# Eight PSUM tiles of one bank in place of four of two, in a kernel of causal attention and a two-layer feed-forward net

## The chip, the core and the metric

The program runs on one core of a Trainium2 chip. Its time is the device time of one execution in microseconds (us), median of three runs. Five engines work side by side, each through a queue of its own in the order written: TensorE (PE in the profile, its weight loads PEld), VectorE (DVE), ScalarE (ACT), GpSimd (POOL) and SyncE (SP, which here only issues DMAs). PSUM, where TensorE writes, has eight banks of 512 float32 columns in each of 128 partitions.

## What is computed

Eight batches, eight heads, 576 tokens, head size 64. Per head: scores `q k^T / 8` plus a decay `cum[s] - cum[t]` (`cum` is the running sum of `log f`), causal mask, softmax over the keys, times `v`. The heads side by side are the 4608 x 512 matrix x of the net:

```python
h = x @ w_in                                        # 512 x 2048
g = np.maximum(h, 0.0) + alpha * np.minimum(h, 0.0)
return (g @ w_out).astype(np.float32)               # 2048 x 512
```

All float32. The large products are made from a high and a low part of each factor (three matmuls of kind fp32r, called the three terms below).

## The kernel before

**Pairs of heads.** The 64 heads are done as 32 pairs n, the two heads of a pair in the two halves of the partitions. Pairs 0 to 9 (`attention`, line 546) turn their weights with TensorE. Pairs 10 to 31 (`turned`, line 800) turn them with VectorE and DMAs. The 576 queries are four blocks of 128 (i = 0 to 3) and a tail of 64; the tails of both heads share one block of 128 rows.

**A turned pair.** TensorE first makes the scores of blocks 3, 2 and 0 of both heads (`run1`, line 850) into four banks: `bA` holds block 3, one bank for each head, `bB` blocks 2 and 0 of a head in one bank. `shrink` (832) follows for each block and head: on VectorE one pass adds the decay and finds the row's minimum (line 840; its accumulator is then read by a short instruction), on ScalarE `expo` makes the exponentials and their sum (820). Then `run2` (873) makes the tail (two halves of 288 keys in the two banks of `bD`) and block 1 (256 columns in each bank of `bC`), again followed by two `shrink` and by `tail` (889; 576 columns in one VectorE pass, line 891). Right behind `run2` TensorE runs `values` (915) of an earlier pair: the product of its turned weights with v, which is x of that pair before division. Its blocks 0 to 3 (t < 4, two batches of 256 columns) go to columns 256 to 511 of the two banks of `bC`, beside block 1 of the present pair, and its tail (t = 4, 64 columns) to columns 320 to 383 of a bank of `bD`, beside the present tail. ScalarE copies x out (938, 940). `turn` (861) is the VectorE transpose of the weights, in two pieces (line 863), and sixteen DMAs (line 900) move the pieces on.

**The net.** `ffn1` (995) multiplies 512 tokens with 128 columns of `w_in`: 12 matmuls of 512 columns into one bank, issued as two halves of six. The bank is emptied by ScalarE (line 1015, or 1012 for the token groups 0, 7 and 8, where that is all) and then by VectorE (1017), and a DMA stores the result (1019). Its matmuls fill TensorE's time between the steps of the pairs. `ffn2` (1224) runs at the end: 18 units of 256 tokens, each with four banks of its own, made by seven products in place of eight and put together by ScalarE and VectorE (lines 1298 to 1315). w_out is converted for it between the pairs' end and its start (1169).

**Banks and order.** The pool of PSUM is four tiles of two banks (line 254); `banks` is a store of the eight halves, and rings (`rS`, `rT`, `rH`, `rO`, `rV`) take single banks from it, each with a least and a most number that it may hold. `rH` (for `ffn1`) holds 2 to 4. When the last plain pair is through, `swap_banks` (1071) claims banks 0 to 3, and whole tiles of two go to the ring `rP` of the turned pairs; `change` (1118) gives them back behind the last pair. The order of all instructions is made by a planner (`Plan.run`, 143): every operation has an assumed duration, a key and its dependencies; the operation with the earliest possible start of all engines is written next (lines 153 to 180), and takes the bank that has been free for longest. The waits between the engines are put in afterwards by the framework, from the accesses to each tile in the order written.

```python
two_banks = [psum.tile([128, 2, 512], F32, name=f"bank{i}") for i in range(4)]
banks = Store([t[:, i] for t in two_banks for i in range(2)])
...
rP, rV = Ring(pairs), Ring(banks, 0, 2)
```

Of the kernel before, what the change touches and what calls it, by code (L numbers as in the profile page):

```python
# [48 lines left out]
class Store:  # L49


    def __init__(self, items):
        self.items, self.rings = items, []
        self.free = [(0.0, i) for i in range(len(items))]
        self.claimed = None

    def take(self):

        f = min(self.free)
        self.free.remove(f)  # L60
        return f

    def give(self, t, i):

        if self.claimed and i in self.claimed[0]:
            self.claimed[1](t, i)
        else:
            self.free.append((t, i))

    def claim(self, which, fn):  # L70

        self.claimed = (which, fn)
        mine, self.free = [f for f in self.free if f[1] in which], [f for f in self.free if f[1] not in which]
        for t, i in mine:
            fn(t, i)

# [34 lines left out]
class Plan:  # L111
# [31 lines left out]
    def run(self):  # L143
# [7 lines left out]
        while left:  # L151
# [40 lines left out]
            for b in o.bufs:  # L192
                if b.t is not None:
                    continue
                st = b.ring.store
                f = st.take()
                b.i, b.t = f[1], st.items[f[1]]
                if o.eng == "PE" and st is self.banks:
                    new.append((f[0], b.t))
                b.ring.next += 1  # L200
                b.ring.held += 1
# [3 lines left out]
            for b in o.bufs:  # L205
                b.left -= 1
                b.last = max(b.last, end)
                if b.left == 0:
                    b.ring.held -= 1
                    b.ring.store.give(b.last + 0.3, b.i)  # L210
            for c in o.outs:
# [7 lines left out]
def attention_moe(  # L219
# [33 lines left out]
    psum = ctx.enter_context(tc.tile_pool(name="psum", bufs=1, space=PSUM))  # L253
    two_banks = [psum.tile([128, 2, 512], F32, name=f"bank{i}") for i in range(4)]
    banks = Store([t[:, i] for t in two_banks for i in range(2)])
    pairs = Store([])
    plan.banks = banks
# [11 lines left out]
    rH, rO = Ring(banks, 2, 4), Ring(banks, 0, 6)  # L269
    rP, rV = Ring(pairs), Ring(banks, 0, 2)  # L270
    rx = Ring(Store([xx[:, 1024 * i : 1024 * i + 1024].rearrange("p (k q) -> p k q", k=2) for i in range(7)]))
# [528 lines left out]
    def turned(n):  # L800
# [8 lines left out]
        bE1, bE2, bTt, bM, bst, bxs, bri = Buf(rE), Buf(rE2), Buf(rEt), Buf(rM), Buf(rst), Buf(rxs), Buf(rri)  # L809
        lo, su = (lambda: bst.t[:, 16:25]), (lambda: bst.t[:, 0:9])  # L810
        sums, turns, moves, x_in = [], [], [], []
# [33 lines left out]

        bA, bB = Buf(rP), Buf(rP)
        t3 = lambda h: bA.t[:, h]
        t2, t0 = (lambda h: bB.t[:, h, 0:384]), (lambda h: bB.t[:, h, 384:512])

# [5 lines left out]
        ns = 250 + c_row(512, 3) + c_row(384, 3) + c_row(128, 3)  # L855
        s = op("PE", ns, run1, k0, rdy, [bA, bB] + held)
        for i, t, bank in ((3, t3, bA), (2, t2, bB), (0, t0, bB)):
            for h in range(2):
                shrink(i, h, lambda t=t, h=h: t(h), k0 + 0.1 * (4 - i), s, bank)

# [8 lines left out]

        bC, bD = Buf(rP), Buf(rP)  # L870
        t1 = lambda h: bC.t[:, h, 0:256]

        def run2():
            for g in range(2):
                for c, (q, k) in enumerate(terms):
                    mm(bD.t[:, g, 0:288], q()[:, 512:640], k()[:, 288 * g : 288 * g + 288], c == 0, c == 2)
            both(1, t1)

        ns = 250 + c_row(256, 3) + 6 * c_mm(288)
        s = op("PE", ns, run2, k0 + 5, rdy, [bC, bD] + held)  # L880
        if len(behind) > 1:
            fn, vd, vb, done = behind.pop(0)(bC, bD)
            done(op("PE", ns_v, fn, k0 + 5.01, [s] + vd, [bC, bD] + vb))
        for h in range(2):
            shrink(1, h, lambda h=h: t1(h), k0 + 5.1, s, bC)

        e5 = lambda: bE2.t[:, 128 * (TAIL - CUT) : 128 * (TAIL - CUT) + S]

        def tail():
            g2 = lambda ap: ap.rearrange("p (g x) -> p g x", g=2)  # L890
            ve.tensor_tensor_reduce(out=g2(e5()), in0=bD.t[:, :, 0:288], in1=g2(bZ.t[1]),
                                    scale=-0.125, scalar=3.0e38, op0=ALU.add, op1=ALU.min, accum_out=lo()[:, 4:5])

        r_ = op("DVE", c_dve(S) + 80, tail, k0 + 5.2, [s, rt], [bD, bE2, bst, bZ])
        expo(bE2, e5, S, 4, k0 + 5.2, [r_])
# [18 lines left out]

        def values(bC, bD):

            def pv():
                m = bM.t
                seen = set()
                for t in (0, 1, 2, 3, 4):  # L920
                    n_ = min(t, 4) + 1
                    for j in range(n_):
                        for h in range(2):
                            if t < 4:
                                o = bC.t[64 * h : 64 * h + 64, t // 2, 256 + 128 * (t % 2) : 384 + 128 * (t % 2)]
                                b0 = 32 * (PLACE[t, h] + j)
                                r = m[:, :, b0 : b0 + 32]
                            else:
                                o = bD.t[64 * h : 64 * h + 64, 0, 320:384]
                                b0 = 32 * (TAIL + j)  # L930
                                r = m[:, 2 * h : 2 * h + 2, b0 : b0 + 32]
                            z = (min(t, 4) // 2, h)
                            mm(o, bv.t[:, j, h], r, z not in seen, j == n_ - 1 and t in (1, 3, 4))
                            seen.add(z)

            def done(o):
                key = k0 + 25.5
                x_in.append(op("ACT", c_act(512), lambda: ac.activation(  # L938
                    bxs.t[:, 0:512].rearrange("p (a n) -> p a n", a=2), bC.t[:, :, 256:512], AF.Copy), key, [o], [bC, bxs]))
                x_in.append(op("ACT", c_act(64), lambda: ac.activation(bxs.t[:, 512:S], bD.t[:, 0, 320:384], AF.Copy), key, [o], [bD, bxs]))  # L940
                value_ops.append(o)
                quotient(n, bxs, bri, x_in + ri_ops, k0 + 26)
# [128 lines left out]
    def swap_banks():  # L1071
        swap((rE.store, [e_1]), (rE2.store, [e_2]))
        got = {}

        def collect(t, i):
            if i ^ 1 in got:
                pairs.free.append((max(t, got[i ^ 1]), len(pairs.items)))
                pairs.items.append(two_banks[i // 2])
            got[i] = t

        rS.least = 0
        banks.claim(range(4), collect)

# [34 lines left out]
    def change():  # L1118
# [8 lines left out]
        for i in range(NW - NV):  # L1127
            wot[i] = p1.tile([128, 2, 7, 256], F32R, name=f"wot{i}")
        banks.claimed = None
        banks.free += [(plan.t, i) for i in range(4)]  # L1130

# [252 lines left out]
```

## Time and profile before

| what | value |
|---|---|
| median of three runs (lowest to highest) | 1138.97 us (1137.51 to 1138.98) |
| the profiled execution | 1137.49 us, span 1135.6 us |
| busy in the span | PE 92%, DVE 70%, ACT 55%, POOL 37% |
| pairs 0 to 9 | about 0 to 205 us |
| the 22 turned pairs, with `ffn1` between | about 205 to 603 us |
| the rest of `ffn1`, conversion of w_out | about 603 to 756 us |
| `ffn2` | about 756 us to the end |

The span goes from the first to the last instruction, and the execution's own time is 1.9 us longer. A PE that is busy need not be at its peak, since the matmuls overlap and their ends are modelled. An idle time in brackets in a timeline is that of the engine just before the instruction, with what ended it.

### The profile page before, as it was taken

Reading aid. Unit: us, or ns where it says so; the run is one execution under the profiler, and the core shown is the slowest. Engines: PE = TensorE matmul, PEld = TensorE weight load, DVE = VectorE, ACT = ScalarE, POOL = GpSimd, SP = SyncE. Lnnn points to the kernel's source line nnn. Section 1 sums busy time; section 2 is a strip of 40 time slices with the busy share of each in tenths; the row PEclk is TensorE's granted clock in tenths of the full one; section 3 lists DMA queues with packets and bytes.
Section 4 is the critical chain, followed back from the end, with each engine's and each line's share of the span. In section 5 each row is a group of like instructions: output and inputs, shape, how many; then the busy total and the mean of one; then the engine's idle time right before and its main releaser. Section 6 shows DMA issues by size and latency. Waiting matters only on the chain. (4 is left out here: it accounts for less than half of the span.)

```text
span 1135.6 us, 22161 instructions
## 1 busy us (share of the span) xinstructions
PE 1049.9 (92%) x7937; PEld 906.2 (80%) x7937; DVE 794.0 (70%) x1651; ACT 619.5 (55%) x1390; POOL 421.9 (37%) x660
## 2 busy tenths in 40 slices
PE   7888998989999898989998898899999999999998
PEld 4577777767778777777876676679999999999998
DVE  4566765467676766667663676549889889899885
ACT  4667786545556555555653464455545454546452
POOL 5366675567786868678664000000000000000000
PEclk9888999999999999999999999999999999999999
DMA  5574854386767768676666445445343334344421
GB/s 158 161 212 148 244 180 136 109 218 191 228 214 229 221 200 239 198 234 209 197 196 204 151 174 183 170 152 161 115 146 115 120 123 149 114 130 130 132 74 38
DMA packets 130064, 190.27 MB, mean 168 GB/s; under 512 B 21841, under 2 KB 78978, under 8 KB 129954
## 3 DMA queue, kind: packets, MB, share of 16 engines
q1 hardware_dynamic: 124034, 170.62, 48.2%
q0 software_dynamic: 5632, 18.03, 5.9%
q8 instruction: 63, 1.03, 0.4%
q14 instruction: 47, 0.39, 0.1%
q10 hardware_dynamic: 288, 0.20, 0.1%
HBM read 103.52 MB, written 48.78 MB: 134 GB/s over the span
## 5 line engine op out<-in xcount | busy, mean ns | idle before, releaser
L377 PE MATMUL bank<-xx,wi 128*128 128x512 f32 x1728 | 428.5, 399 | 50.1 <-DVE hs L1017 25.0
L377 PEld LDWEIGHTS bank<-xx,wi 128*128 128x128 f32 x1728 | 317.0, 189 | 135.9 <-DVE hs L1017 32.2
L1017 DVE SCALAR_TENSOR_TENSOR hs<-bank,sa,hs 128x512 f32<-128x512 f32 x96 | 71.2, 742 | 108.8 <-ACT hs L1015 69.4
L820 ACT ACTIVATE big<-big,st 128x512 f32<-128x512 f32 (+4 forms) x198 | 114.0, 577 | 52.9 <-DVE st L840 52.9
L1015 ACT ACTIVATE hs<-bank,ab 128x512 f32<-128x512 f32 x96 | 65.9, 688 | 129.6 <-PE bank L377 99.0
L377 PE MATMUL bank<-wot,xx 128*128 128x256 f32 x1008 | 125.5, 284 | 3.4 <-DVE hs L1303 1.7
L377 PEld LDWEIGHTS bank<-wot,xx 128*128 128x128 f32 x1008 | 122.5, 192 | 5.0 <-DVE hs L1303 2.1
L377 PE MATMUL bank<-wi,xx 128*128 128x256 f32 x1008 | 123.9, 283 | 0.0
L377 PEld LDWEIGHTS bank<-wi,xx 128*128 128x128 f32 x1008 | 122.3, 192 | 0.0
L539 POOL TENSOR_TENSOR Qhl<-rqk,Qhl 128x640 fp32r<-128x640 f32 (+1 forms) x56 | 85.0, 1525 | 95.3 <-ACT Qhl L538 95.3
L377 PE MATMUL bank<-Qhl 64*128 64x128 f32 (+4 forms) x840 | 96.7, 330 | 8.4 <-DVE st L697 5.1
L377 PEld LDWEIGHTS bank<-Qhl 64*128 64x128 f32 (+1 forms) x840 | 79.1, 188 | 30.5 <-issue 7.3
L377 PE MATMUL bank<-big,vr 128*64 128x128 f32 (+2 forms) x1880 | 97.1, 262 | 0.8 <-ACT xs L938 0.8
L377 PEld LDWEIGHTS bank<-big,vr 128*64 128x64 f32 x1880 | 90.2, 139 | 8.8 <-issue 2.6
L900 POOL DMA_DIRECT2D big<-big x176 | 88.2, 508 | 0.9 <-issue 0.9
L863 DVE STREAM_TRANSPOSE big<-big 128x2048 f32<-128x2048 f32 (+1 forms) x44 | 79.8, 1826 | 3.3 <-DMA hd<-hs 1.9
L840 DVE CUSTOM_DVE_ANT_1 big<-bank,Z 128x384 f32<-128x384 f32 (+1 forms) x88 | 39.6, 487 | 48.0 <-PE bank L377 48.0
L512 POOL TENSOR_TENSOR Z<-Z,tri 128x384 f32<-128x384 f32 x64 | 60.7, 955 | 31.8 <-DMA Z<-c 16.3
L1272 ACT ACTIVATE xx<-gx 128x1024 fp32r<-128x1024 f32 x48 | 50.8, 1058 | 38.1 <-DVE gx L1259 22.3
L1012 ACT ACTIVATE hs<-bank,sg 128x512 f32<-128x512 f32 x48 | 33.0, 688 | 59.4 <-PE bank L377 50.7
L377 PE MATMUL bank<-wot,gh 128*128 128x256 f32 x504 | 63.6, 284 | 1.5 <-DVE hs L1303 0.8
L377 PEld LDWEIGHTS bank<-wot,gh 128*128 128x128 f32 x504 | 61.6, 192 | 2.6 <-DVE hs L1303 1.1
(151 smaller groups left out, 1594.8 us busy)
## 6 DMA issues: line engine op xcount, KB each, us to landing
hd<-hs SPq DMA_DIRECT2D x144, 256.0 KB, 2.6
wx<-hd SPq DMA_DIRECT2D x47, 512.0 KB, 3.4
big<-big SPq DMA_DIRECT2D x176, 100.0 KB, 4.3
big<-big POOLq DMA_DIRECT2D x176, 100.0 KB, 4.5
rqk<-in_qk_dram SPq DMA_DIRECT2D x28, 608.0 KB, 4.8
hr<-hd SPq DMA_DIRECT2D x25, 512.0 KB, 4.0
vr<-in_vv_dram SPq DMA_DIRECT2D x32, 320.0 KB, 3.1
big<-in_w_in_dram SPq DMA_DIRECT2D x16, 512.0 KB, 4.6
```

What stands on the lines that cost most here:

```text
L377: pe.matmul(o, lhsT, rhs, start=start, stop=stop)
L512: m1 = op("POOL", c_po(128 * 3), lambda z4=z4: po.tensor_tensor(z4()[:, 6:9], z4()[:, 0:3], tb(3), ALU.add), kc + 0.1, got + [o_mask], [bZ])
L539: o2 = op("POOL", c_po(w), lambda hi=hi, lo=lo, raw=raw: po.tensor_tensor(lo(), raw(), hi().bitcast(F32), ALU.subtract), kc, [o1], [bqk, bQ])
L820: sums.append(op("ACT", c_exp(w), lambda: ac.activation(at(), at(), AF.Exp, bias=lo()[:, col : col + 1], scale=-1.0, accum_out=su()[:, col ...
L840: ve.tensor_tensor_reduce(out=blk(e()), in0=blk(src()), in1=in1, scale=-0.125, scalar=3.0e38, op0=ALU.add, op1=ALU.min, accum_out=lo()[:, ...
L863: turns.append(op("DVE", c_tr(4 * (c1 - c0)), lambda: ve.transpose(bTt.t[:, :, c0:c1].rearrange("p k (b c) -> p k b c", c=32), bE.t.rearra ...
L900: moves.append(op(n_, 550 if i % 2 else 450, lambda a=a, k=k, q_=q_: q_.dma_start(bM.t[32 * k : 32 * k + 32, a], bTt.t[32 * a : 32 * a + 3 ...
L1012: cp = op("ACT", c_act(512), lambda bh=bh, bs=bs, fc=fc: ac.activation(bs.t, bh.t, AF.Copy, scale=sg[:, fc : fc + 1]), -1000, [last, o_sg] ...
L1015: cp = op("ACT", c_act(512), lambda bh=bh, bs=bs, fc=fc: ac.activation(bs.t, bh.t, AF.Relu, scale=ab[:, fc : fc + 1]), -1000, [last, o_sg] ...
L1017: cp = op("DVE", c_dve(512), lambda bh=bh, bs=bs, fc=fc: ve.scalar_tensor_tensor(bs.t, bh.t, sa[:, fc : fc + 1], bs.t, ALU.mult, ALU.add), ...
L1272: his.append(op("ACT", c_acs(128 * GW * (j1 - j0)), lambda j0=j0, j1=j1, src=src, o_=o_: ac.activation(o_(0, j0, j1), src(), AF.Copy), key ...
```

## The change

The pool becomes eight tiles of one bank, and `rP` a ring of single banks: at most four, and at least four from the swap to `change`. The claim of fixed banks is gone, so the turned pairs and `ffn1` now take from all eight, the longest free one first. In a turned pair `bA`, `bB` and `bC` are two buffers each, `bD` is one, and `bX` is new. The tail's 576 keys become a part of 320 (in `bD`) and one of 256 (in `bC[0]`, columns 256 to 511, beside block 1 of head 0), so its minimum takes two VectorE passes, the second beginning with the minimum of the first. x of the earlier pair has `bX` for its blocks 0 to 3, and its 64 tail columns go to `bC[1]`, beside block 1 of head 1. Block 1 of head 1 is now shrunk before that of head 0, and both stand ahead of `values` in the text of the function.

```diff
 class Store:
...
-    def claim(self, which, fn):
...
-    two_banks = [psum.tile([128, 2, 512], F32, name=f"bank{i}") for i in range(4)]
-    banks = Store([t[:, i] for t in two_banks for i in range(2)])
-    pairs = Store([])
+    banks = Store([psum.tile([128, 512], F32, name=f"bank{i}") for i in range(8)])
...
-    rP, rV = Ring(pairs), Ring(banks, 0, 2)
+    rP, rV = Ring(banks, 0, 4), Ring(banks, 0, 2)
...
-        lo, su = (lambda: bst.t[:, 16:25]), (lambda: bst.t[:, 0:9])
+        lo, su = (lambda: bst.t[:, 16:26]), (lambda: bst.t[:, 0:9])
...
-        bA, bB = Buf(rP), Buf(rP)
-        t3 = lambda h: bA.t[:, h]
-        t2, t0 = (lambda h: bB.t[:, h, 0:384]), (lambda h: bB.t[:, h, 384:512])
+        bA, bB = ([Buf(rP), Buf(rP)] for _ in range(2))
+        t3 = lambda h: bA[h].t
+        t2, t0 = (lambda h: bB[h].t[:, 0:384]), (lambda h: bB[h].t[:, 384:512])
...
-        bC, bD = Buf(rP), Buf(rP)
-        t1 = lambda h: bC.t[:, h, 0:256]
+        bC, bD, bX = [Buf(rP), Buf(rP)], Buf(rP), Buf(rP)
+        t1 = lambda h: bC[h].t[:, 0:256]
+        part = ((0, 320, lambda: bD.t[:, 0:320]), (320, S, lambda: bC[0].t[:, 256:512]))
 
         def run2():
-            for g in range(2):
+            for c0, c1, out in part:
                 for c, (q, k) in enumerate(terms):
-                    mm(bD.t[:, g, 0:288], q()[:, 512:640], k()[:, 288 * g : 288 * g + 288], c == 0, c == 2)
+                    mm(out(), q()[:, 512:640], k()[:, c0:c1], c == 0, c == 2)
             both(1, t1)
...
-        s = op("PE", ns, run2, k0 + 5, rdy, [bC, bD] + held)
+        s = op("PE", ns, run2, k0 + 5, rdy, bC + [bD, bX] + held)
+        for h in (1, 0):
+            shrink(1, h, lambda h=h: t1(h), k0 + 5.1, s, bC[h])
         if len(behind) > 1:
-            fn, vd, vb, done = behind.pop(0)(bC, bD)
-            done(op("PE", ns_v, fn, k0 + 5.01, [s] + vd, [bC, bD] + vb))
-        for h in range(2):
-            shrink(1, h, lambda h=h: t1(h), k0 + 5.1, s, bC)
+            fn, vd, vb, done = behind.pop(0)(bX, bC[1])
+            done(op("PE", ns_v, fn, k0 + 5.01, [s] + vd, [bX, bC[1]] + vb))
...
-        def tail():
-            g2 = lambda ap: ap.rearrange("p (g x) -> p g x", g=2)
-            ve.tensor_tensor_reduce(out=g2(e5()), in0=bD.t[:, :, 0:288], in1=g2(bZ.t[1]),
-                                    scale=-0.125, scalar=3.0e38, op0=ALU.add, op1=ALU.min, accum_out=lo()[:, 4:5])
-
-        r_ = op("DVE", c_dve(S) + 80, tail, k0 + 5.2, [s, rt], [bD, bE2, bst, bZ])
+        r_ = None
+        for g, (c0, c1, src) in enumerate(part):
+            def tail(g=g, c0=c0, c1=c1, src=src):
+                ve.tensor_tensor_reduce(out=e5()[:, c0:c1], in0=src(), in1=bZ.t[1][:, c0:c1], scale=-0.125,
+                                        scalar=lo()[:, 9:10] if g else 3.0e38, op0=ALU.add, op1=ALU.min,
+                                        accum_out=lo()[:, 4:5] if g else lo()[:, 9:10])
+
+            r_ = op("DVE", c_dve(c1 - c0) + 80, tail, k0 + 5.2, [s, rt, r_], [bC[0] if g else bD, bE2, bst, bZ])
...
-                                o = bC.t[64 * h : 64 * h + 64, t // 2, 256 + 128 * (t % 2) : 384 + 128 * (t % 2)]
+                                o = bX.t[64 * h : 64 * h + 64, 128 * t : 128 * t + 128]
...
-                                o = bD.t[64 * h : 64 * h + 64, 0, 320:384]
+                                o = bY.t[64 * h : 64 * h + 64, 256:320]
...
     def swap_banks():
         swap((rE.store, [e_1]), (rE2.store, [e_2]))
...
         rS.least = 0
-        banks.claim(range(4), collect)
+        rP.least = 4
...
-        banks.claimed = None
-        banks.free += [(plan.t, i) for i in range(4)]
+        rP.least = 0
```

## Rows read from the trace of the kernel before

**Rows 1.** The page, engines: busy us (share of the span) and instructions

```profile
PE 1049.9 (92%) x7937; PEld 906.2 (80%) x7937; DVE 794.0 (70%) x1651; ACT 619.5 (55%) x1390; POOL 421.9 (37%) x660
```

**Rows 2.** Stretches: their length, busy us (instructions) by engine, PEclk, DMA share, GB/s

```profile
0.00:205.00 205.00, 178.15 (x1368) 136.58 (x1370) 122.72 (x314) 139.46 (x375) 127.73 (x190) 0.93 0.57 173
205.00:603.00 398.00, 367.99 (x2929) 299.74 (x2926) 265.87 (x604) 222.81 (x582) 283.52 (x457) 1.00 0.70 208
603.00:756.00 153.00, 133.08 (x604) 102.78 (x602) 83.68 (x144) 67.75 (x103) 10.66 (x16) 1.00 0.49 165
756.00:1136.00 380.00, 370.67 (x3042) 367.09 (x3042) 321.69 (x589) 189.49 (x332) 0.00 (x0) 1.00 0.39 123
```

**Rows 3.** Waits of PEld, 205 to 603 us: total us, times, longest

```profile
PEld bank L377 <- DVE hs L1017: 23.6, 18, 2.1
PEld bank L377 <- ACT hs L1015: 12.1, 10, 1.2
PEld bank L377 <- ACT xs L938: 7.7, 16, 1.2
```

**Rows 4.** Waits of PEld, 603 to 756 us

```profile
PEld bank L377 <- ACT hs L1012: 15.7, 13, 1.2
PEld bank L377 <- DVE hs L1017: 8.7, 5, 2.0
PEld bank L377 <- ACT hs L1015: 3.6, 3, 1.2
```

**Rows 5.** Waits of PEld, 756 us to the end

```profile
PEld bank L377 <- DVE hs L1303: 3.2, 3, 1.1
PEld bank L377 <- DVE hs L1302: 2.7, 4, 0.7
```

**Rows 6.** Timeline, 660 to 710 us, PE and ACT: start, us, engine, line

```profile
665.36 5.78 PE L377 MATMUL bank<-xx,wi 128*128 128x512 f32 x24 [0.78 <-ACT hs L1012]
667.07 0.69 ACT L1012 ACTIVATE hs<-bank,sg 128x512 f32<-128x512 f32 x1 [1.76 <-PE bank L377]
...
671.17 0.69 ACT L1012 ACTIVATE hs<-bank,sg 128x512 f32<-128x512 f32 x1 [1.98 <-PE bank L377]
...
671.91 5.78 PE L377 MATMUL bank<-xx,wi 128*128 128x512 f32 x24 [0.78 <-ACT hs L1012]
```

**Rows 7.** Timeline of PE, two stretches without a break between 704 and 723 us

```profile
704.73 11.17 PE L377 MATMUL bank<-xx,wi 128*128 128x512 f32 x48 [0.83 <-ACT hs L1012]
716.73 5.73 PE L377 MATMUL bank<-xx,wi 128*128 128x512 f32 x24 [0.83 <-ACT hs L1012]
```

**Rows 8.** Timeline, 614 to 616 us, DVE and PE

```profile
614.59 0.75 DVE L1017 SCALAR_TENSOR_TENSOR hs<-bank,sa,hs 128x512 f32<-128x512 f32 x1 [3.33 <-ACT hs L1015]
615.39 1.67 PE L377 MATMUL bank<-xx,wi 128*128 128x512 f32 x6 [1.56 <-DVE hs L1017]
```

**Rows 9.** Timeline, 434 to 441 us, a turned pair: values, block 1, x, next run1

```profile
434.38 2.99 PE L377 MATMUL bank<-big,vr 128*64 128x128 f32 x60
...
436.83 0.42 DVE L840 CUSTOM_DVE_ANT_1 big<-bank,Z 128x256 f32<-128x256 f32 x1 [3.58 <-PE bank L377]
...
439.63 0.58 ACT L938 ACTIVATE xs<-bank 128x512 f32<-128x512 f32 x1
...
440.26 1.64 PEld L377 LDWEIGHTS bank<-Qhl 64*128 64x128 f32 x18 [0.37 <-ACT xs L938]
```

**Rows 10.** Waits of DVE, 205 to 603 us

```profile
DVE big L840 <- PE bank L377: 51.6, 21, 3.6
```

**Rows 11.** Lines 891 and 607: minimum of the tail in one pass and in two

```profile
L891 DVE CUSTOM_DVE_ANT_0 big<-bank,Zt x22: 745/753/754, 223.7 to 597.0; 128x576 f32<-128x576 f32 x22
...
L607 DVE CUSTOM_DVE_ANT_0 big<-bank,Zt x10: 445/452/459, 16.8 to 187.1; 128x288 f32<-128x288 f32 x10
L607 DVE CUSTOM_DVE_ANT_0 big<-bank,Zt,st x10: 457/518/519, 17.4 to 187.6; 128x288 f32<-128x288 f32 x10
```

**Rows 12.** Waits of PE, 0 to 205 us, the largest

```profile
PE bank L377 <- DVE st L697: 7.3, 7, 2.3
```

More of the change, by code (lines that the diff above doesn't have):

```diff
@@ L54, in __init__ @@
         self.free = [(0.0, i) for i in range(len(items))]
[L55 to L68, printed above, removed]
-    def claim(self, which, fn):
[L72 to L75, printed above, removed]
 class Ring:
@@ L195, in run @@
                 st = b.ring.store
-                f = st.take()
+                f = min(st.free)
+                st.free.remove(f)
                 b.i, b.t = f[1], st.items[f[1]]
@@ L209, in run @@
                     b.ring.held -= 1
-                    b.ring.store.give(b.last + 0.3, b.i)
+                    b.ring.store.free.append((b.last + 0.3, b.i))
             for c in o.outs:
@@ L855, in turned @@
         ns = 250 + c_row(512, 3) + c_row(384, 3) + c_row(128, 3)
-        s = op("PE", ns, run1, k0, rdy, [bA, bB] + held)
+        s = op("PE", ns, run1, k0, rdy, bA + bB + held)
         for i, t, bank in ((3, t3, bA), (2, t2, bB), (0, t0, bB)):
             for h in range(2):
-                shrink(i, h, lambda t=t, h=h: t(h), k0 + 0.1 * (4 - i), s, bank)
+                shrink(i, h, lambda t=t, h=h: t(h), k0 + 0.1 * (4 - i), s, bank[h])
         def turn(bE, b0, b1, key, deps):
@@ L913, in turned, with values @@
             d[:, 128 * h : 128 * h + 160].rearrange("(o a) n -> o a n", o=1).broadcast_to([64, 4, 160])), k0 + 8.2, [st_], [bri], kb=160) for h in range(2)]
-        def values(bC, bD):
+        def values(bX, bY):
             def pv():
@@ L928, in pv @@
                             else:
-                                o = bD.t[64 * h : 64 * h + 64, 0, 320:384]
+                                o = bY.t[64 * h : 64 * h + 64, 256:320]
                                 b0 = 32 * (TAIL + j)
                                 r = m[:, 2 * h : 2 * h + 2, b0 : b0 + 32]
-                            z = (min(t, 4) // 2, h)
-                            mm(o, bv.t[:, j, h], r, z not in seen, j == n_ - 1 and t in (1, 3, 4))
+                            z = (t // 4, h)
+                            mm(o, bv.t[:, j, h], r, z not in seen, j == n_ - 1 and t in (3, 4))
                             seen.add(z)
@@ L937, in done @@
                 key = k0 + 25.5
-                x_in.append(op("ACT", c_act(512), lambda: ac.activation(
-                    bxs.t[:, 0:512].rearrange("p (a n) -> p a n", a=2), bC.t[:, :, 256:512], AF.Copy), key, [o], [bC, bxs]))
-                x_in.append(op("ACT", c_act(64), lambda: ac.activation(bxs.t[:, 512:S], bD.t[:, 0, 320:384], AF.Copy), key, [o], [bD, bxs]))
+                x_in.append(op("ACT", c_act(512), lambda: ac.activation(bxs.t[:, 0:512], bX.t, AF.Copy), key, [o], [bX, bxs]))
+                x_in.append(op("ACT", c_act(64), lambda: ac.activation(bxs.t[:, 512:S], bY.t[:, 256:320], AF.Copy), key, [o], [bY, bxs]))
                 value_ops.append(o)
@@ L1072, in swap_banks @@
         swap((rE.store, [e_1]), (rE2.store, [e_2]))
[L1073 to L1079, printed above, removed]
         rS.least = 0
-        banks.claim(range(4), collect)
+        rP.least = 4
     o_swap = op("-", 0, swap_banks, 0, last_e)
```

## The prediction, made before the changed kernel ran

> **What bounds the kernel now.** I read the page's engines first: TensorE is busy for 92% of the span, and the next, VectorE, for 70% [rows 1]. Then the stretches: from 205 us to the end TensorE is 87 to 98% busy at the full granted clock, and in the pairs' stretch nothing else is near it: VectorE 265.9, GpSimd 283.5 of 398 us, DMA a share of 0.70 [rows 2]. So TensorE's gaps are the time that can be had, and I ask the waits of its weight loads, stage by stage, for what ends them; the loads run ahead of the matmuls, so their idle time shows a stop more fully than that of the matmuls, whose modelled ends cover part of it. In the pairs' stretch it is the emptying of `ffn1`'s banks: 23.6 us on VectorE's line 1017 and 12.1 us on ScalarE's 1015 [rows 3]. Behind the pairs it is the same, 15.7, 8.7 and 3.6 us [rows 4], and in `ffn2` the adding up of a unit's banks, 3.2 and 2.7 us [rows 5].
>
> What kind of wait is it? The reader should look at the rhythm in the rest of `ffn1`. TensorE does exactly 24 matmuls, two banks' worth, and stops for 0.78 us, which is one ScalarE emptying of 0.69 us and the handing over [rows 6]. The emptyings begin 1.71 us after a restart and again at its end, 5.81 us after it [rows 6]: that is behind six matmuls and behind all 24 (at the pace worked out below, 1.4 and 5.4 us and then the drain), not behind 12 and 24, where banks become full. This fits a wait for the neighbour in the same tile of two banks. The planner writes half a bank's matmuls of the neighbour ahead of the emptying of the first bank; the emptying then waits for these matmuls, and the neighbour's second half waits for the emptying. The other tile, next in turn, gives 18 free matmuls, and it begins again. Where VectorE empties too, the stop is 1.56 us, and TensorE starts 0.05 us behind VectorE's end at 615.34 [rows 8]. A lack of banks would not do this: here `ffn1` has four banks, and the bank just filled is the one that TensorE waits for.
>
> The Trainium skill (PSUM — Partial Sum Buffer, the section on bank collisions) says that two engines may work on different banks at once, while on one bank and the same partitions they must be kept apart whatever the columns. By that rule none of these stops is owed to the chip; the rows above agree in so far as the stop has the period of the tile and not of the bank. Another rule of the skill (Perfetto Trace Analysis, Optimization Strategy) speaks against the change: the same gap repeating on the engine that should be full can mean too little PSUM. The change adds no bank, so by it nothing would be gained; that is the second rival.
>
> **Part one: eight tiles.** It removes no instruction, only these waits. The pace without a break is (11.17 - 5.73) / 24 = 0.227 us a matmul of 512 columns [rows 7]. From one restart to the next are 6.55 us for 24, which need 5.44, so a stop loses 1.11 us [rows 6], against 15.7 / 13 = 1.21 us of idle weight loads [rows 4]: I count 92% of that idle time. Pairs' stretch 35.7 us, rest of `ffn1` 28.0, `ffn2` 5.9: together 69.6, times 0.92 is **64 us**. What is late next? A pair's period is 398 / 22 = 18.1 us and would become 16.6. Per pair VectorE is busy 12.1, GpSimd 12.9, the DMA engines 12.7 us [rows 2], all below 16.6, so I keep the whole of it for the forecast. In the rest of `ffn1` VectorE has 83.7 us of work in 153 [rows 2], which fits in 127, and the converted w_out follows the same matmuls. In `ffn2` VectorE goes from 321.7 in 380 to 321.7 in 374, still below TensorE.
>
> In pairs 0 to 9 TensorE stands for 205 - 178 = 27 us [rows 2]. The largest part names the minimum of the scores [rows 12], a real link of the chain, though it may itself have waited for a neighbour bank. The trace can't part the two: the bounds are 0 and 27 us. I take **6**, nearer to none, since nothing here has the rhythm of the neighbour.
>
> **Part two: x in a bank of its own.** Now block 1 waits for x: VectorE starts it 2.45 us into the 2.99 us of `values`, when the blocks 0 to 3 of x, which lie beside it in `bC`, are done [rows 9]. VectorE loses 51.6 us so in 21 waits [rows 10]. One would think that this goes. It doesn't: the 64 tail columns of x now lie in `bC[1]`, beside block 1 of head 1, and that block is the first that VectorE takes. The planner writes the earliest start first: `values` can start when `run2` ends, the minimum only a handing over later, so `values` is still written ahead, whatever the order of the function's text. Block 1 of head 1 then waits for the last matmuls of `values`: the full 2.9 us and the same handing over of about 0.3, some 0.7 us later than now. Queued behind it on VectorE are block 1 of head 0, both parts of the tail, the turning and `ffn1`'s emptyings; ScalarE's exponentials and copy of x wait for these. VectorE's own slack, 18.1 - 12.1 - 51.6 / 22 = 3.7 us a pair now and 16.6 - 12.1 - 3.1 = 1.4 afterwards, covers it, so I take 0. Without that cover it is 0.7 x 22 = 15 us. If the blocks are written ahead after all, VectorE gets the 2.3 us a pair back, which shows in TensorE's time only through the waits already counted: no gain beyond them.
>
> Next, `run1` waits for the copy of x, 7.7 us in 16 waits [rows 3], 0.37 us in the pair shown [rows 9]. With eight banks in one store the longest free is taken, often one that `ffn1` left, so this can go: bounds from 7.7 gained to 0.9 x 22 = 20 lost (the copy is late by the 0.7 and the tail's 0.2). I take 0, by the rows that show it mostly a small one.
>
> **Part three: the tail in two passes.** Now 0.753 us; two passes of 288 take 0.452 + 0.518 = 0.970 [rows 11], so about 0.22 us more of VectorE a pair, 5 us in all, 22 passes and 22 readings of an accumulator. It lies in the same slack: 0, and 5 without the cover. The tail's matmuls stay six a pair with the same 1728 columns, x has the same matmuls, its copy the same 512 columns: 0. No DMA is added or moved in the text; SP's and GpSimd's queues keep their work and follow the plan.
>
> **Sum.** 64 + 6 = 70 us off the profiled execution's 1137.5 (span 1135.6 and 1.9 around it) is 1067.5; the median of the runs is 1.5 higher, so **1069 us**.
>
> **Rivals.** (1) *VectorE takes over the pairs' stretch.* Its chain through a pair gets 0.9 us longer where TensorE's gets shorter; if the turning and the sixteen moves behind it set the period, only the gain outside the pairs is left: 33.9 x 0.92 = 31 us, **1108 us**. For it: each pair must finish its minimum before `run2` can have its banks. Against: the slack of 1.4 us. Chance 0.13. (2) *The stops are a lack of banks*, or the framework's waits stay for another reason; the change doesn't do what it says. Then 64 becomes 0, and with the 0 to 5 us of the tail hidden or not it stays at **1139 us**. Against: the rhythm. Chance 0.03. (3) *Slower: the copy of x holds `run1`.* Place: TensorE's queue in front of `run1`, behind it all of `ffn1`; price 0.9 us in 22 pairs, 20 us; with none of the waits gone **1159 us**. It decides as soon as the waits of part one give back less than 20 us. For it: 16 pairs already wait there. Chance 0.05. The forecast has 0.79.
>
> **How the numbers follow.** The forecast's own case goes from 64 + 27 + 8 = 99 us gained (1040) to about 64 + 0 - 20 = 44 (1095). The range reaches towards the first rival: **1040 to 1105**, which leaves out about 2 in 10: rivals 2 and 3, most of rival 1 and the thin ends. 0.2% (2.3 us) is what a measurement of this kernel can tell from no change. Faster are the forecast and rival 1: 0.92; same 0.03; slower 0.05.
>
> **What would show it.** Right: the rest of `ffn1` runs in one stretch without a stop each 24 matmuls, emptyings 2.7 us apart; the rows on lines 1012, 1015 and 1017 as TensorE's releasers nearly gone; `ffn2` without the stops on 1302 and 1303; line 840 with 256 columns starting about 3.2 us behind `run2`. Wrong: stops of 0.78 and 1.56 us still there (rival 2), or in their place waits of TensorE for line 840 or the copy of x (rivals 1 and 3).

## The result, and the profile after

The changed kernel takes **1038.87 us** (median of 4 runs, 1035.94 to 1042.32) against 1138.47 (1137.51 to 1138.98) for the kernel before beside it: a ratio of 0.9127, 95% interval 0.9098 to 0.9156. The gain is 100 us. The prediction was 1069, its range 1040 to 1105: the direction and the mechanism held, the size did not, and the time fell just below the range.

The page's engines, after:

```profile
PE 1017.0 (98%) x7937; PEld 898.2 (87%) x7937; DVE 809.5 (78%) x1695; ACT 615.7 (59%) x1390; POOL 424.7 (41%) x660
```

The stretches, after (columns as in [rows 2]; the boundaries are where this kernel goes from one stage to the next):

```profile
0.00:170.00 170.00, 161.72 (x1352) 125.12 (x1352) 131.45 (x313) 136.27 (x373) 130.52 (x189) 1.00 0.69 209
170.00:543.00 373.00, 365.48 (x3003) 305.34 (x3003) 271.25 (x649) 221.32 (x585) 287.78 (x464) 1.00 0.79 226
543.00:670.00 127.00, 127.00 (x569) 105.15 (x565) 86.80 (x146) 70.01 (x105) 6.36 (x8) 1.00 0.56 194
670.00:1037.00 367.00, 362.82 (x3024) 362.61 (x3022) 319.97 (x587) 188.08 (x328) 0.00 (x0) 1.00 0.39 125
```

TensorE is the limit almost alone now, busy for 98% in place of 92% [rows 1]. To see where the time came from I take two marks from TensorE's timeline, the first `run1` of a turned pair and the first matmul of `ffn2`:

| | start to first `run1` | to first `ffn2` matmul | to the end of the span |
|---|---|---|---|
| before | 207.4 | 552.9 | 375.3 |
| after | 170.1 | 499.7 | 366.8 |
| gained | **37.2** | **53.3** | **8.5** |
| predicted | 6 | 58.6 | 5.4 |

The marks in the timelines, before (line 377) and after (line 355):

```profile
207.36 1.78 PE L377 MATMUL bank<-Qhl 64*128 64x512 f32 x18
760.27 5.21 PE L377 MATMUL bank<-wot,gh 128*128 128x256 f32 x42
```

```profile
170.14 1.77 PE L355 MATMUL bank<-Qhl 64*128 64x512 f32 x18
669.79 5.20 PE L355 MATMUL bank<-wot,gh 128*128 128x256 f32 x42
```

The middle and the end are near their terms ((35.7 + 28.0) x 0.92 = 58.6, and 5.9 x 0.92 = 5.4). Pairs 0 to 9 gained six times theirs.

**The rest of `ffn1`.** TensorE's timeline, and ScalarE's emptyings in a part of it:

```profile
543.17 126.78 PE L355 MATMUL bank<-xx,wi 128*128 128x512 f32 x558
```

```profile
642.79 0.69 ACT L992 ACTIVATE hs<-bank,sg 128x512 f32<-128x512 f32 x1 [0.50 <-PE bank L355]
645.51 0.69 ACT L992 ACTIVATE hs<-bank,sg 128x512 f32<-128x512 f32 x1 [2.03 <-PE bank L355]
```

558 matmuls run without a break, where there was a stop behind each 24 [rows 6]; the pace is 126.78 / 558 = 0.227 us, the one worked out from [rows 7]. Two emptyings follow each other in 2.72 us, one bank's worth.

**The pairs' stretch.** Waits of TensorE's weight loads from 170 to 543 us, the largest:

```profile
PEld bank L355 <- issue: 6.0, 8, 3.3
PEld bank L355 <- DVE st L871: 5.2, 14, 0.4
PEld bank L355 <- POOL xx L949: 3.0, 2, 1.9
PEld bank L355 <- DVE st L818: 2.0, 2, 1.4
PEld bank L355 <- DVE hs L997: 1.7, 2, 1.2
```

The emptyings of `ffn1` cost 1.7 us where they cost 23.6 and 12.1 [rows 3]; from 543 us on this view is empty, so the stops of `ffn2` [rows 5] are gone too. The 14 rows that name the tail's second pass (line 871) stand ahead of `run1`, and they are no wait for it. Two of the `run1` after the change:

```profile
183.44 1.65 PEld L355 LDWEIGHTS bank<-Qhl 64*128 64x128 f32 x18 [0.35 <-issue]
...
232.46 1.63 PEld L355 LDWEIGHTS bank<-Qhl 64*128 64x128 f32 x18 [0.37 <-DVE st L871]
```

All 22 of them have this idle time of the loads, 0.35 to 0.37 us, whether the row names line 871, another line or nobody ("issue"), and TensorE's matmuls run through. Before, 19 of the 22 had it as well (0.35 to 0.38 us), most of them under the name of the copy of x [rows 9].

**x's own bank.** Timeline around one `values` (423.88 is `run2`, 425.32 `values`), and VectorE's largest wait in the stretch:

```profile
423.88 1.50 PE L355 MATMUL bank<-Qhl 128*128 128x320 f32 x12
...
425.32 2.99 PE L355 MATMUL bank<-big,vr 128*64 128x128 f32 x60
...
428.38 0.42 DVE L818 CUSTOM_DVE_ANT_1 big<-bank,Z 128x256 f32<-128x256 f32 x1 [1.33 <-PE bank L355]
```

```profile
DVE big L818 <- PE bank L355: 35.0, 20, 4.2
```

Block 1 begins 3.06 us into `values`, 0.6 later than before [rows 9], as foretold: x's tail beside block 1 of head 1 holds it. Of the 51.6 us of waiting [rows 10] 35.0 are left.

**Pairs 0 to 9.** Written out for both kernels, the planner's list of operations begins with the same 949 in the same order; the next one is the first `run1` in the changed kernel, while the kernel before has eleven others ahead of its own. Over these 949 only the tiles differ. TensorE's largest waits ahead of it, before (the first of them is [rows 12]) and after:

```profile
PE bank L584 <- ACT big L580: 4.1, 5, 1.3
PE bank L584 <- DVE st L697: 2.9, 4, 1.1
PE bank L377 <- ACT big L580: 2.1, 2, 1.2
PE bank L377 <- DVE st L607: 1.9, 1, 1.9
```

```profile
PE bank L562 <- ACT big L558: 2.1, 3, 1.6
PE bank L415 <- DVE big L412: 1.4, 1, 1.4
PE bank L627 <- ACT wi L350: 1.3, 2, 0.7
PE bank L562 <- DVE st L675: 1.2, 2, 0.7
```

The 7.3 us behind the minimum of [rows 12] is gone, so it was in the main a wait for the neighbour after all. One of the seven, before, and the same six matmuls after:

```profile
186.17 0.69 ACT L1012 ACTIVATE hs<-bank,sg 128x512 f32<-128x512 f32 x1 [0.29 <-PE bank L377]
...
186.97 0.44 PE L377 MATMUL bank<-Qhl 64*128 64x384 f32 x1
...
188.62 0.69 DVE L697 CUSTOM_DVE_ANT_0 big<-bank,Z 128x512 f32<-128x512 f32 x1
...
189.37 0.80 PE L377 MATMUL bank<-Qhl 64*128 64x384 f32 x5 [1.97 <-DVE st L697]
```

```profile
157.67 1.19 PE L355 MATMUL bank<-Qhl 64*128 64x384 f32 x6
...
158.07 0.47 PEld L355 LDWEIGHTS bank<-Qhl 64*128 64x128 f32 x5 [0.22 <-ACT hs L992]
```

The first of the six goes through and the second stands for 1.97 us, until VectorE has read a minimum of other scores. The planner's list has the banks: the second matmul writes bank 3, which `ffn1` had left at 186.86 (line 1012), and the minimum at 188.62 reads bank 2, the other half of the tile. After the change the only wait named there is for the emptying of bank 3 itself (line 992).

There was a second loss, which I had not looked at: the granted clock. Before, in five stretches (the sum of the lengths is 27.3 us), it was at the lower of its two levels, 1.2 GHz:

```profile
36.80:43.60 6.80, 5.50 (x28) 4.41 (x26) 1.91 (x9) 3.94 (x15) 3.15 (x7) 0.50 0.86 245
57.30:60.70 3.40, 3.40 (x18) 3.40 (x18) 2.17 (x5) 2.64 (x7) 2.31 (x2) 0.50 1.07 282
74.30:77.80 3.50, 3.50 (x17) 2.85 (x16) 1.97 (x11) 2.77 (x11) 2.54 (x4) 0.51 0.84 234
91.40:101.60 10.20, 8.82 (x37) 7.01 (x36) 9.07 (x20) 7.01 (x20) 10.20 (x8) 0.50 0.22 61
190.40:193.80 3.40, 3.40 (x46) 3.40 (x43) 0.00 (x0) 1.27 (x4) 0.00 (x0) 0.50 0.20 74
```

After, no such stretch lies ahead of the first `run1`: 1.00 over 0 to 170 us, above.

### The profile page after: what moved, and what is told of

It reads as the page before. It is cut to its first block, busy times and chain, and to the rows that moved or that the text cites. A ratio compares the mean times of both kernels' runs of the same rounds, so it can differ in the third digit from the quotient of the medians.

```text
span 1036.6 us, 22203 instructions
## 1 busy us (share of the span) xinstructions
PE 1017.0 (98%) x7937; PEld 898.2 (87%) x7937; DVE 809.5 (78%) x1695; ACT 615.7 (59%) x1390; POOL 424.7 (41%) x660
## 4 chain that ended last, share of the span: by engine, by line
PE 77%; DVE 9%; POOL 4%; SPq 3%; DMA 2%; issue 2%; ACT 1%; DVEq 0%; POOLq 0%; ACTq 0%
PE bank L355 75%; DVE big L841 3%; SPq L881 3%; PE bank L562 1%; DVE big L818 1%; DMA rd<-st 1%; POOL Z L490 1%; POOL wi L351 1%; DVE big L346 1%; POOL Qhl L517 1%; DVE Z L474 1%; DMA hd<-hs 1%; DMA ri<-rd 1%; PE bank L415 1%; DVE hs L997 1%
## 5 line engine op out<-in xcount | busy, mean ns | idle before, releaser
L355 PE MATMUL bank<-xx,wi 128*128 128x512 f32 x1728 | 413.4, 394 | 2.2 <-POOL xx L949 2.2
L517 POOL TENSOR_TENSOR Qhl<-rqk,Qhl 128x640 fp32r<-128x640 f32 (+1 forms) x56 | 87.8, 1574 | 35.0 <-ACT Qhl L516 33.9
L355 PE MATMUL bank<-Qhl 64*128 64x128 f32 (+6 forms) x840 | 94.1, 326 | 2.1 <-DVE st L818 1.2
L1246 DVE TENSOR_TENSOR xx<-gx,xx 128x1024 fp32r<-128x1024 f32 x48 | 58.5, 1219 | 8.0 <-ACT xx L1243 8.0
L355 PE MATMUL bank<-wi,gh 128*128 128x256 f32 x504 | 62.4, 283 | 0.0
```

The source lines that it names most:

```text
L355: pe.matmul(o, lhsT, rhs, start=start, stop=stop)
L517: o2 = op("POOL", c_po(w), lambda hi=hi, lo=lo, raw=raw: po.tensor_tensor(lo(), raw(), hi().bitcast(F32), ALU.subtract), kc, [o1], [bqk, bQ])
L1246: rdy.append(op("DVE", c_dve(128 * GW * (j1 - j0)), lambda j0=j0, j1=j1, src=src, o_=o_: ve.tensor_tensor(o_(1, j0, j1), src(), o_(0, j0, ...
```

## Experiments

Two theories to begin with. *Theory 1*: the waits for the neighbour in a two-bank tile are everything; x's own bank and the new places do little. *Theory 2*: x's own bank, or the free choice among eight, carries a large part. The kernel before ran beside each batch of experiments, with a median of 1136.3 to 1138.5 us; the ratios are to it.

**x back beside block 1.** The changed kernel with its eight tiles, but x again in columns 256 to 511 of the two banks of block 1, and the tail as 288 and 288 keys in two banks (the text of the function has `values` ahead of the two `shrink` again, too):

```diff
-        bC, bD, bX = [Buf(rP), Buf(rP)], Buf(rP), Buf(rP)
+        bC, bD = ([Buf(rP), Buf(rP)] for _ in range(2))
...
-            fn, vd, vb, done = behind.pop(0)(bX, bC[1])
+            fn, vd, vb, done = behind.pop(0)(bC, bD[0])
...
-                                o = bX.t[64 * h : 64 * h + 64, 128 * t : 128 * t + 128]
+                                o = bX[t // 2].t[64 * h : 64 * h + 64, 256 + 128 * (t % 2) : 384 + 128 * (t % 2)]
```

> Eight tiles of one bank and the shared ring stay; x of the earlier pair goes back beside block 1 (both banks of bC, its tail beside the present tail), the tail is two passes of 288, x is copied in three pieces. Theory 1 (the waits for the neighbour in the tile are everything, x's own bank nothing): 1035 to 1050 us, pairs 0 to 9 as short as in the changed kernel (first run1 at about 170 us), block 1's minimum about 2.4 us behind run2. Theory 2 (x's own bank carries the gain in the turned pairs): the 56 us of that part are mostly lost, 1070 us or more.

Measured: 1040.75 us, ratio 0.9154 (0.9133 to 0.9175), an interval that overlaps that of the change. As it stands, x's own bank is worth nothing that can be measured; the first `run1` starts at 169.3 us here, too.

**Fixed banks for the turned pairs**, the changed kernel with banks 0 to 3 claimed for them as before, though each a tile:

```diff
-    rP, rV = Ring(banks, 0, 4), Ring(banks, 0, 2)
+    pairs = Store(banks.items)
+    pairs.free = []
+    rP, rV = Ring(pairs), Ring(banks, 0, 2)
...
+        banks.claimed = range(4)
```

> The changed kernel, but the turned pairs get banks 0 to 3 for themselves again, ffn1 the other four. Theory 1 (the waits for the neighbour are everything): 1037 to 1052 us; run1 waits for the copy of x again, about 0.4 us in most pairs, up to 8 us in all. Theory 2 (the free choice of eight banks carries part of the gain): 1060 us or more, with TensorE waiting in the pairs for lines of the minimum or of ffn1's emptying.

Measured: 1050.04 us, ratio 0.9232 (0.9215 to 0.9250), in theory 1's range but not for its reason: the copy of x is named for 1.2 us only. The free choice among eight is worth some 11 us. The weight loads' largest wait in its pairs' stretch shows where:

```profile
PEld bank L359 <- DVE st L875: 11.8, 17, 2.0
```

With four banks of its own, a pair's `run1` waits up to 2.0 us for the tail's second pass of the pair before, in the middle of its 18 matmuls; the changed kernel has no such stop.

**Alternate halves.** The kernel before, with its two-bank tiles, but the store hands out the first halves of the four tiles and then the second ones, so that banks taken one behind the other are not neighbours:

```diff
-    banks = Store([t[:, i] for t in two_banks for i in range(2)])
+    banks = Store([t[:, i] for i in range(2) for t in two_banks])
...
-        banks.claim(range(4), collect)
+        banks.claim((0, 1, 4, 5), collect)
```

> The kernel before with its four tiles of two banks; only the order in which the store hands out the eight halves is changed (first halves of the four tiles, then the second halves), so that banks taken one after the other are of different tiles. Theory 1 (neighbour in the tile): most stops in ffn1 go, 1050 to 1100 us, the stop of 0.78 us each 24 matmuls in the rest of ffn1 gone or rare; pairs 0 to 9 only in part. Theory 2 (four banks for ffn1 are too few): no change, 1136 to 1141 us, stops as before.

Measured: 1108.71 us, ratio 0.9753 (0.9732 to 0.9775), above my 1100 by a little. 28 us against the 1136.26 beside it come from the order in which the same banks of the same tiles are taken (the planner's list changes with it, behind its first 949 operations), so the stops are not a property of the number of banks. The rhythm in the rest of `ffn1` changes with it:

```profile
663.49 16.66 PE L377 MATMUL bank<-xx,wi 128*128 128x512 f32 x72 [0.78 <-ACT hs L1012]
680.97 5.73 PE L377 MATMUL bank<-xx,wi 128*128 128x512 f32 x24 [0.83 <-ACT hs L1012]
687.53 16.61 PE L377 MATMUL bank<-xx,wi 128*128 128x512 f32 x72 [0.83 <-ACT hs L1012]
```

Two stops in 96 matmuls, where there were four: a part of the waits stays as long as tiles of two are shared.

**Three banks for `ffn1`.** The changed kernel, with at most three where it had four. This was meant to test the rule of the rival: a shortage should come back.

```diff
-    rH, rO = Ring(banks, 2, 4), Ring(banks, 0, 6)
+    rH, rO = Ring(banks, 2, 3), Ring(banks, 0, 6)
```

> The changed kernel with at most three banks for ffn1 in place of four. Theory 1 (what stopped TensorE before was the neighbour in the same tile, three banks of one tile each are enough to fill one while one is emptied): 1038 to 1043 us, the rest of ffn1 still without a stop of over 0.5 us. Rival (the old stops were a shortage of banks, and the change helped by giving ffn1 a free choice among eight): 1053 us or more, with stops behind the emptyings again.

Measured: 1038.30 us, ratio 0.9122 (0.9097 to 0.9147); beside it the changed kernel had 0.9128. But the edit does nothing: in the changed kernel's list `ffn1` never holds more than three banks (one or two in 139 of the 144 times that it takes one), so the limit is never reached, and the two programs are the same, instruction for instruction. The run repeats the changed kernel and tests no theory.

What speaks against a shortage is the list of the kernel before. There `ffn1` holds one or two banks in 137 of 144 times and four only once; in the rest of `ffn1` it goes through all eight and not through four, and by the plan the one it takes next has been free for 8 us or more. The alternate halves say the same. The Trainium skill (Perfetto Trace Analysis, Optimization Strategy) reads a gap that repeats on the engine that should be full as a possible lack of room for the next tile; here it was the same room, cut into fewer tiles than there were users.

**x's tail behind the minimum.** The changed kernel with `values` in two pieces, the second (t = 4, the 64 tail columns in `bC[1]`) made to follow the minimum of block 1 of head 1:

```diff
-            done(op("PE", ns_v, fn, k0 + 5.01, [s] + vd, [bX, bC[1]] + vb))
+            o = op("PE", ns_v - 5 * c_m4(64) - 125, lambda fn=fn: fn((0, 1, 2, 3)), k0 + 5.01, [s] + vd, [bX] + vb)
+            done(op("PE", 5 * c_m4(64) + 125, lambda fn=fn: fn((4,)), k0 + 5.02, [o, mins[0]], [bC[1]] + vb))
```

> The changed kernel, but the matmuls of values are two operations and those of x's tail (t = 4, into the bank of block 1 of head 1) depend on that block's minimum, so they are written behind it. Theory 1 (block 1 waits for values because they are written ahead; VectorE has slack): the minimum of block 1 starts within 0.5 us behind run2 where VectorE is free, VectorE's 35 us of waits on line 818 nearly vanish, the time moves by no more than 4 us (1035 to 1041). Theory 2 (VectorE's chain paces the pairs): 10 us or more faster than the changed kernel, below 1030 us.

Measured: 1033.25 us, ratio 0.9080 (0.9057 to 0.9104), between the two theories. To part 5.6 us from the difference of two batches, it ran once more beside the changed kernel:

> The changed kernel itself once more, beside the next one on the same chip: 1036 to 1042 us by every theory.

> The kernel with values in two pieces once more, beside the changed kernel on the same chip. Theory 1 (block 1 of head 1 waited for the tail of x, 35 us of VectorE's time in 20 waits, and a part of this reached TensorE): 4 to 8 us below the changed kernel. Rival (the 5.6 us seen between two chips were the chips): within 2 us of it.

Measured: 1038.96 us (1037.44 to 1041.91) and 1032.84 us (1031.97 to 1034.40), ratios 0.9128 and 0.9073. The runs do not overlap; the 6 us are real, and this version beats both kernels. In its trace block 1 hardly waits for x any more. Timeline around one `values`, and the wait that was 35.0 us:

```profile
419.75 1.50 PE L355 MATMUL bank<-Qhl 128*128 128x320 f32 x12
...
421.19 2.98 PE L355 MATMUL bank<-big,vr 128*64 128x128 f32 x60
...
422.49 0.42 DVE L818 CUSTOM_DVE_ANT_1 big<-bank,Z 128x256 f32<-128x256 f32 x1
```

```profile
DVE big L818 <- PE bank L355: 7.8, 8, 1.2
```

The middle stage (first `run1` at 171.0, first `ffn2` matmul at 664.6 us) takes 493.6 us, 6.1 less than after the change, and TensorE's matmuls stand for 2.5 us of it where they stood for 7.5. So x's own bank does pay, once nothing else of x stands in a bank that VectorE wants first. How the late block 1 reached TensorE is only argued: the waits that went name several lines, and the planner's list differs behind the first 1165 operations.

**The tail's two passes alone**, in the kernel before:

```diff
-        r_ = op("DVE", c_dve(S) + 80, tail, k0 + 5.2, [s, rt], [bD, bE2, bst, bZ])
+            r_ = op("DVE", c_dve(288) + 80, tail, k0 + 5.2, [s, rt, r_], [bD, bE2, bst, bZ])
```

> The kernel before with one part of the change alone: the tail's minimum in two VectorE passes of 288 keys, both from the two-bank tile. The prediction took 0, with 5 us as the bound without cover. Theory 1 (VectorE has the slack, or what it is late by hides behind the neighbour waits): 1136 to 1141 us. Rival (the 0.2 us a pair come through in all 22 pairs): 1143 us or more.

Measured: 1133.31 us, ratio 0.9966 (0.9948 to 0.9984), a little faster, below the range of either theory. The extra VectorE work costs nothing that shows. The planner writes another order from the first turned pair on, and the middle stage shrinks by 4.5 us; which step of that order pays is open.

This run also gives the tiles a test by themselves. Its list and that of the kernel with fixed banks begin with the same 2772 operations of 4152, up to the end of the pairs, though one has four tiles of two banks and the other eight of one. The first takes 1133.31 us (0.9966), the second 1050.04 (0.9232). So 83 of the 100 us come with the smaller tiles in nearly the same order of work; the places of x and of the tail differ too, but these moved nothing that could be measured above.

**The dummy matmuls.** In the first 75 us the planner fills TensorE's planned waits with 84 dummy matmuls. I left them out of the changed kernel, and then of the kernel before (`FILL = 75.0` becomes `FILL = 0.0`), to price the clock:

> The 84 dummy matmuls that fill TensorE's planned waits in the first 75 us are left out; all else is the changed kernel's. They lie in waits that are there anyway, so by themselves they cost no time. Theory 1 (pairs 0 to 9 gained 37 us in two ways: fewer stops, and a full clock because there were fewer stops): with the fillers gone TensorE stands longer, the granted clock falls to about 0.5 in some stretches of the first 75 us, and each such us costs up to half of itself: first run1 of a turned pair at 175 to 185 us in place of 170, time 1044 to 1054 us. Rival (the clock plays no part, all 37 us were stops): first run1 at 169 to 172 us, time 1036 to 1041 us.

Measured: 1038.67 us, ratio 0.9125 (0.9099 to 0.9151); first `run1` at 166.8 us. TensorE did stand longer (it was busy for 93.0 us of the first 100 with the dummies), but its clock did not fall:

```profile
0.00:100.00 100.00, 87.62 (x718) 63.08 (x719) 79.79 (x206) 78.94 (x222) 74.52 (x121) 1.00 0.76 220
```

So this didn't test what it was made for. Both expectations missed the first `run1`; the time is in the rival's range, and what was gained at the first `run1` does not reach the end. That gain is 1.6 to 3.3 us: three profiles of the changed kernel's program have it at 170.1, 168.5 and 168.6.

> The kernel before, without the 84 dummy matmuls in the first 75 us. Each of them is written into the bank that the next real matmul will take, so with tiles of two banks a dummy can itself wait for the neighbour. Theory 1 (in the kernel before they run behind a neighbour wait and not in it, and add their 0.12 to 0.28 us each to the path): 3 to 12 us faster, first run1 at 195 to 204 us in place of 207. Rival (they hold the clock up, and without them it falls for longer): 3 to 12 us slower, with over 27 us at a granted clock near 0.5 ahead of the first run1. Both at once may leave it within 3 us; then the granted clock and the idle time in the trace tell the two parts.

Measured: 1134.05 us, ratio 0.9966 (0.9947 to 0.9986); first `run1` at 203.9 us, with 34 us near 0.5 ahead of it. Both things happened: the clock was low for 7 us longer, and the start came 3.5 us earlier. In the kernel before the dummies cost a little time, then; whether they wait for neighbours is open, since the start came 1.6 to 3.3 us earlier without neighbours, too, and three profiles of the kernel before differ by 2.2 us there (table below).

**The price of half clock.** The kernel with two passes writes the same order as the kernel before ahead of the first `run1`, but its profile had fewer stretches at half clock. Two more executions of the kernel before were profiled to get a line from such pairs of numbers:

> The kernel before, unchanged, looked at once more: the first of two looks to price the half clock. Its first profile had 27.3 us at a granted clock near 0.5 ahead of the first run1 of a turned pair, which started at 207.4 us; the kernel with the tail's minimum in two passes has the same order up to there, had 17.0 us and started at 205.0. Theory 1 (a us at half clock costs about 0.25 us): this look lies within 1 us of 207.4 + 0.25 x (its us at half clock - 27.3). Rival (half a us, by the busy time): within 1 us of the same line with 0.5.

> The second such look: the same two lines, 0.25 or 0.5 us for a us at half clock, from 207.4 us at 27.3 us.

Measured, the same instructions in the same order each time:

| profile of | us at half clock | first `run1` |
|---|---|---|
| two passes | 17.0 | 205.0 |
| kernel before, second profile | 20.5 | 205.1 |
| kernel before, third profile | 23.9 | 206.9 |
| kernel before, first profile | 27.3 | 207.4 |

The line with 0.25 gives 205.7 and 206.5 for the two new profiles, the one with 0.5 gives 204.0 and 205.7: the first holds within 1 us, the second misses by 1.1 and 1.2. That is little to tell them apart by, and the 0.25 was drawn from the other two points. The recorded runs say more: over 39 executions of the kernel before, with mean granted clocks from 0.983 to 0.991, the span grows by 0.37 us (95% interval 0.28 to 0.45) for each us at half clock that its mean clock stands for (twice what the mean lacks to 1, times the span), and over the ten of the kernel with two passes by 0.34. So both lines miss, and the 27.3 us cost about 10, an estimate from 27.3 x 0.37. The Trainium skill (TensorE: Matmul & The Clock Gate, HAM oscillation) takes half of the time spent at half rate, which would be 13.7 us; here about three quarters of that show, and a reason is in sight though not tested: the work in these stretches stands partly ahead of waits that would have been there at full clock.

## Why the prediction was wrong, and where it was right

**The step that failed** is the term for pairs 0 to 9: "I take 6, nearer to none, since nothing here has the rhythm of the neighbour", with bounds of 0 and 27 us. It measured 37.2. About 4 of these are no saving, but 62 matmuls (six of `ffn1` and a `values` of 56) that the new order puts behind the first `run1`. With the same work done, the two kernels stand here, before and after (columns as in [rows 2]):

```profile
0.00:203.00 203.00, 176.15 (x1353) 135.11 (x1354) 121.97 (x313) 137.85 (x373) 125.73 (x187) 0.93 0.57 175
```

```profile
0.00:170.14 170.14, 161.86 (x1353) 125.12 (x1354) 131.45 (x313) 136.27 (x373) 130.66 (x189) 1.00 0.69 209
```

The other 33 us are the tiles, since neither the order nor the work differs up to there. The kernel with fixed banks agrees: it has the list of the kernel before up to and past the first `run1` and comes to it at 172.8 us, 34.6 earlier. Of the 33 some 10 are the half clock, by the price above, and the other 23 are stops on the neighbour; this division is an estimate. Three things were wrong in the step:

- *The sign looked for.* The rhythm of 24 matmuls is that of `ffn1`, which takes banks at an even pace. Pairs 0 to 9 take them at an uneven one (scores, turned weights, x and `ffn1` in turn), so the neighbour belongs to whichever user came next, and the wait carries the name of that user's reader: a minimum on 697, an exponential on 580. It looks like a link of the chain. The test that the trace allowed was to ask, for a wait, whether the instruction named reads the bank that the stopped matmul writes; I did not ask it.
- *The upper bound.* 27 us was the idle time of the matmuls, while the other stages were counted by the weight loads, whose idle time I had myself called the fuller measure. Theirs is 207.4 - 138.6 = 68.7 us before and 170.1 - 125.1 = 45.0 after, 24 less, where the matmuls' own fell by 18.6. 92% of the 24, by the prediction's own factor, is 22 us, and with the clock's 10 this comes near the 33.
- *The clock.* [Rows 2] showed 0.93 for this stretch beside 1.00 for the others, and I made no term of it.

With 33 in place of 6 the sum would have been 1042.

**Part one elsewhere** was right in kind. Its size came out near, and this is in part luck: 58.6 us were foretold for the middle and 53.3 came, or 57.6 with the moved matmuls counted where they were before, but other effects are in it. From the kernel with two passes to the one with fixed banks, with nearly the same list, the middle shrinks by 40.6 us (548.4 to 507.8), and the fixed banks have 11.8 us of waits of their own; the free choice takes them away. `ffn2` gave 8.5 in place of 5.4.

**Part two**: the mechanism was right, the size was not. `values` stayed ahead of block 1's minimum, and block 1 started some 0.6 us later than before. But "VectorE's own slack covers it, so I take 0" fell: the version that undoes that wait is 6 us faster. 1.4 us of slack a pair is a mean, and a pair does not come at even times; that this is the reason is argued, not shown. The run without x's own bank lands on the time of the change, so the two halves of the edit, a bank of x's own and x's tail ahead of the first block, seem to have cancelled each other. That the copy of x would cost or give `run1` little held, but the 7.7 us were misread: nearly all of them are the 0.35 to 0.38 us that nearly every `run1` shows in either kernel, so there was next to nothing to gain or to lose.

**Part three** held: no cost.

**The rivals.** VectorE did not take over the pairs' stretch: it is busy for 271 of 373 us, and the gain came through. A shortage of banks is ruled out by the alternate halves and by the planner's list of the kernel before, not by the run that limits `ffn1` to three. The copy of x holds nothing up. What I had only as a bound of 7.7 us, and took at 0, was a gain from the free choice among eight, some 11 us: with banks of their own the pairs have stops at `run1` that the prediction doesn't know.

## What to carry to other kernels

A tile is the unit in which the framework's waits are put in, so a tile of two banks makes two users wait for each other though the banks are separate; cut a pool into tiles as small as what is handed out. Where a wait in a trace names a reader, check that it reads the very bank the stopped writer wants; if it doesn't, the whole wait can go, whatever its rhythm. Where the same short idle time stands at the same place under changing names, it is no wait for any of them. Before a limit is lowered to test for a shortage, check that it is ever reached. And a piece moved out of a shared bank gains only when its last piece is out: look at what the reader takes first.

## What the runs showed that was not expected

The granted clock does not follow the order of instructions alone. The kernel before, unchanged, spent 27.3, 20.5 and 23.9 us at half clock in three profiles, in partly other places (19 to 22 and 25.5 to 29 us in the last alone, 190 to 194 in the first alone). In the first TensorE had been busy for 6.83 and 6.79 us of the two stretches of 10 us ahead of the fall at 36.8; without the dummies the changed kernel stood for 12.4 us of its first 100 and stayed at full clock. What decides it is open, and the price, about 0.37 of the time spent there, holds for this kernel.
